# Scores of the first channel slot in two visits, and the middle angles of the first full theta slot ahead of its rotations

## The chip, the cores and the metric

The kernel runs on one core of a Trainium2 chip. The metric is device time in microseconds (us) for one execution. The kernel before takes 859.88 us, the median of three runs (858.89 to 861.0).

## The reference

```python
def _attn_ref(q, k, v, cap):                      # q, k, v: 8 x 12 heads x 448 x 64
    scores = cap * np.tanh(scale * q @ k.T / cap)
    attn = np.exp(scores - max); attn /= sum + 1e-09
    return attn @ v
def _moe_ref(x, w_theta, w_tok_r, w_tok_i, w_ch): # x: 8 x 448 x 768, the heads side by side
    theta = x @ w_theta
    y = w_tok_r @ (x * cos(theta)) + w_tok_i @ (x * sin(theta))
    u = x + y
    return u + np.maximum(u @ w_ch, 0.0)
```

Attention with capped scores feeds a block that turns each element by an angle `theta`, mixes along the tokens, adds, and ends in a channel matrix with a ReLU.

## The kernel before

Attention is cut into 24 slots of two pairs of heads each, so three slots make up one batch. A slot `s` makes the scores of its two pairs (words `S0` to `S3`), their tanh (`t0` to `t3`) and exp (`e0` to `e3`), and takes from slot `s-1` the product with V (`V0`, `W`, and the rest `Vr`), the row sums (`Ra`, `Rb`), their reciprocals (`I`) and the copies of the product out of PSUM (`cV0`, `cV1`). Into the same slots the second block is woven, four slots behind: a theta slot (`T` the matrix, `y` the angle in turns, `d` its reduction, `sc` sine and cosine, `r` the rotation, `f` a transpose, `D` the DMAs that carry the transposed piece across partitions), a mix slot (`h` and `l` halves of the data, `M` the token matrix, `m` the sum) and a channel slot (`u` halves of the data, `C` the matrix, `c` its output), each for six blocks of 128 channels.

Matrices are multiplied in three products of fp32r halves. The weights of the channel matrix come in twelve pieces, `ch0a` to `ch5b`, during slots 4 to 6: `@` loads a piece by two DMAs on POOL's queue, `*` scales it on ACT, `0` makes three DVE passes (L197, L198, L199), `1` one more DVE pass, and `2` casts the high half on ACT (L203, which waits for L198) and makes the low half on DVE (L204). Then its room goes back, and the load of a later piece that takes this room may start.

The order of the work is written by hand. `OTHER[s]` and `PARTS` are lists of words; `run` executes them one after the other, and this puts each word's instructions at the end of the queue of its engine. Engines run their queues in that order and wait for each other by semaphores. Slot 6 (`LEAD + 2`) is the first channel slot, slot 7 (`LEAD + 3`) the first theta slot behind it, slot 8 a mix slot from `PARTS`. The slots 5 and 6 are also those that split the channel weights.

PSUM has eight banks. Four go around in the pool `psM` (tag `m`) and hold one accumulator each (product, theta, mix, channel, sums); four belong to scores. Up to slot 6 the four are one tile: `S0`, `S1` and `S2` fill it one after the other, and one tanh of 1,792 columns empties it. From slot 7 on (`HALVES`, `once`) they are two tiles of two banks. There `S2` and `S3` take four banks of `psM` and one of the halves, so that all of `S1`, `S2`, `S3` stand in one visit, and the row sums lie in a bank of the score tile that `S1` fills afterwards. There, too, `cV1` runs on DVE instead of ACT, and the k halves of the second pair have rooms of their own.

Steps named later: `sums` (L491), `turn` (transposes the sums out of PSUM), `av_out` (the copies), `scores`, `tanh`, `prep_q`, `prep_k`, and `Split`/`Fields` for weights.

Of the kernel before, what the change touches and what calls it, by code (L numbers as in the profile page):

```python
# [28 lines left out]
LEAD = 4  # L29
# [10 lines left out]

FOLD = (0, 1, 2)

HALVES = LEAD + 3

FILL = {"branch": 10, "S0": 2, "t0": 8, "t1": 4}

# [34 lines left out]
def softcap_attn_then_spectral_mix(ctx, tc, qk2, v, cap, w_theta, w_tok, w_ch, outT):  # L81
# [9 lines left out]
    NS = B * NP2  # L91
# [191 lines left out]

    def once(s):
        return LEAD + 2 < s < NS

    def load_raw(k, part, last=False):
        t = raw[k, part] = small.take([P, S], F32, f"{'qk'[part]}{k}", None, int(part == 0 and once(k // 2) and (k // 2 - LEAD) % NP2 == 2), last)
        nc.sync.dma_start(t, qk2[k // NP, k % NP, :, part, :])
# [5 lines left out]
    def halves(t, shape, room, name, early):  # L295

        out = [room(shape, F32R, f"{name}{part}") for part in "hl"]
        (nc.scalar.copy if early else nc.vector.tensor_copy)(out[0], t)
        nc.vector.tensor_tensor(out[1], t, out[0].bitcast(F32), op=ALU.subtract)
        return out  # L300

    def by_scalar(k):
        return k < 2 * LEAD + 8 or k % 2 == 0 and (k // 2 - LEAD) % NP2 == 2

    def prep_q(k):

        if 2 * WHOLE <= k < 2 * NS:
            Q[k, "q"] = halves(raw[k, 0], [P, S], small.take, f"q{k}", by_scalar(k))
            if once(k // 2) and k % 2 and (k // 2 - LEAD) % NP2:
                Q[k, "rooms"] = [small.take([P, S], F32R, f"k{k}{part}") for part in "hl"]  # L310

    def prep_k(k, early=False):

        if 2 * WHOLE <= k < 2 * NS:
            t = raw[k, 1]
            if once(k // 2) and k % 2:
                if (k, "rooms") not in Q:
                    Q[k, "rooms"] = [small.take([P, S], F32R, f"k{k}{part}") for part in "hl"]
                rooms = iter(Q[k, "rooms"])
                Q[k, "k"] = halves(t[:, :REST], [P, REST], lambda shape, dtype, name: next(rooms)[:, :REST], f"k{k}", by_scalar(k))  # L320
            else:
                Q[k, "k"] = halves(t[:, :REST], [P, REST], lambda shape, dtype, name: wk.tile(shape, dtype, tag=f"k{name[-1]}", name=name, bufs=1), f"k{k}", by_scalar(k))
            if k % 2 == 0:
                Q[k, "r"] = wk.tile([P, S - REST], F32, tag="kr", name=f"r{k}", bufs=1)
                nc.vector.tensor_copy(Q[k, "r"], t[:, REST:])
            if early:
                Q[k, "early"] = True
            else:
                small.give(raw.pop((k, 1)))
            if k + 1 < 2 * NS:  # L330
                load_raw(k + 1, 1, k % 2 == 0 and by_scalar(k) and k > 2 * LEAD + 6)

    def scores(s, n):
        if once(s) and n >= 2:
            t = spt[s, n] = [psM.tile([P, 512], F32, tag="m", name=f"s{s}_{n}{h}") for h in range(2)]
            if n == 3:
                two = spt[s, "u"] = state["scores"].tile([P, 2, 512], F32, tag="s1", name=f"s{s}_u")
                chunk(s, (1, 2), [two[:, h] for h in range(2)])
            chunk(s, (1, n - 2), t)
        elif n == 3 and not once(s) and s not in (1, LEAD + 1):  # L340
            t = spt[s, n] = [psM.tile([P, 512], F32, tag="m", name=f"s{s}_{n}{h}") for h in range(2)]
            chunk(s, (1, 2), t)
        else:
            two = spt[s, n] = state.pop("two", None) if once(s) and n == 1 else None
            if not two:
                two = spt[s, n] = halves_of(s, n)
            for u, what in sorted(enumerate(BURSTS[n]), key=lambda at: at[1] is not None):
                chunk(s, what, [two[0][u][:, h] for h in range(2)])
        k = 2 * s + n // 2
        if n in ((1, 3) if s else (1, 2)) and s < WHOLE:  # L350
            for part in range(2):
                small.give(raw.pop((k, part)))
        elif s >= WHOLE and n % 2:
            for t in Q.pop((k, "q")) + (Q.pop((k, "rooms")) if (k, "rooms") in Q else []):
                small.give(t)
            if n == 1:
                for i in range(2):
                    small.give(raw.pop((k + i, 0)))
                if Q.pop((k + 1, "early"), False):
                    small.give(raw.pop((k + 1, 1)))  # L360
                if k + 2 < 2 * NS:
                    for i in range(2, 4):
                        load_raw(k + i, 0, once(s) and (s - LEAD) % NP2 == 2)

    def chunk(s, what, out):
        for i in (0, 1) if what is None else what[:1]:
            k = 2 * s + i
            rows, cols = (slice(i * D, (i + 1) * D), slice(REST, S)) if what is None else (slice(0, P), slice(what[1] * P, (what[1] + 1) * P))
            if what is None and (k, "r") in Q:
                products = ((Q.pop((k, "r")), raw[k, 0]),)  # L370
            elif what is None or s < WHOLE:
                products = ((raw[k, 1][:, cols], raw[k, 0]),)
            else:
                kk, qq = Q[k, "k"], Q[k, "q"]
                products = [(kk[a][:, cols], qq[c]) for a, c in (((0, 0), (0, 1), (1, 0)) if once(s) and i else ((0, 0), (1, 0), (0, 1)))]
            for m, (kk, qq) in enumerate(products):
                for h in range(2):
                    half = slice(h * D, (h + 1) * D)
                    nc.tensor.matmul(out[h][rows, :S], kk[half], qq[half], start=m == 0, stop=m == len(products) - 1)  # L379
# [317 lines left out]
    def chan_out(b, m):  # L697
# [190 lines left out]
```

## Time and profile before

| | |
|---|---|
| three runs | 858.89, 859.88, 861.0 us |
| profiled execution | 859.83 us, span 858.0 us |
| PE busy | 849.7 us (99% of the span), granted clock 0.999 |
| DVE, ACT, POOL busy | 720.7, 575.9, 116.0 us |
| chain that ended last, share of PE | 95% |

The span is what the trace covers, and the profiled execution's own time is 1.8 us longer. A timeline row gives the start in us, the time in us, the engine, the source line, the operation, output and inputs, and in brackets how long the engine stood idle before it and who released it. Several instructions may be merged in one row (`x8`); its time then runs from the first start to the last end. On one engine an instruction usually starts a little before its forerunner's end is recorded, so that the step from start to start is up to 0.1 us shorter than the recorded time.

### The profile page before, as it was taken

To read this page: it belongs to the slowest core of one execution; us is meant where nothing else is said; L and a number is where in the kernel's file an instruction comes from. 1 tells how busy PE (TensorE), PEld (TensorE's weight loads), DVE (VectorE), ACT (ScalarE), POOL (GpSimd) and SP (SyncE) were. 2 spreads that over 40 slices of the span, in tenths; PEclk is the share of its full clock that TensorE was granted. 3 is DMA by queue.
4 is the path that set the end of the run, shared out by engine and by line. 5 is a ranking of instruction groups with operands and counts; after the bars stand their busy time and mean duration, and the time that the engine had idled before them with its cause. 6 is when DMAs were issued, how large, how long until landed. Compare 5 with 4: busy or idle time off the path is not lost.

```text
span 858.0 us, 13327 instructions
## 1 busy us (share of the span) xinstructions
PE 849.7 (99%) x4756; PEld 646.1 (75%) x4756; DVE 720.7 (84%) x1168; ACT 575.9 (67%) x730; POOL 116.0 (14%) x244
## 2 busy tenths in 40 slices
PE   9999999999999999999999999999999999999997
PEld 4335676867878779778787797787787877879996
DVE  5988989999889898879998798897989979876741
ACT  6898987786873778727868468655787377824420
POOL 1121242201300032000310013000130003200300
PEclk9999999999999999999999999999999999999999
DMA  8686275741422324322423324134142332411401
GB/s 315 198 299 227 71 239 192 258 130 43 130 80 86 116 65 130 97 97 65 125 81 97 113 67 122 55 119 130 44 130 82 92 95 62 111 44 33 141 13 57
DMA packets 51692, 99.74 MB, mean 116 GB/s; under 512 B 11232, under 2 KB 42208, under 8 KB 51616
## 3 DMA queue, kind: packets, MB, share of 16 engines
q1 hardware_dynamic: 38880, 58.81, 22.1%
q0 software_dynamic: 9568, 29.89, 11.4%
q10 hardware_dynamic: 3168, 10.09, 3.9%
q8 instruction: 39, 0.64, 0.3%
q14 instruction: 37, 0.30, 0.1%
HBM read 54.72 MB, written 11.01 MB: 77 GB/s over the span
## 4 chain that ended last, share of the span: by engine, by line
PE 95%; DVE 2%; ACT 1%; issue 0%; SPq 0%; DMA 0%; ACTq 0%; POOL 0%; DVEq 0%; POOLq 0%
PE s L379 13%; PE a L483 13%; PE mx L684 8%; PE mx L686 8%; PE mx L685 8%; PE ch L583 7%; PE ch L584 7%; PE ch L585 7%; PE th L583 6%; PE th L585 6%; PE th L584 6%; PE a L477 2%; PE r L521 2%; PE s_u L379 1%; ACT p L405 1%; PE fill L130 1%
## 5 line engine op out<-in xcount | busy, mean ns | idle before, releaser
L653 POOL DMA_DIRECT2D t<-g_row x160 | 78.7, 499 | 531.5 <-ACT z L607 424.9
L684 PE MATMUL mx<-wtk_h,zh 128*128 128x448 f32 x336 | 124.1, 369 | 0.0
L686 PE MATMUL mx<-wtk_h,zl 128*128 128x448 f32 x336 | 123.4, 367 | 0.1
L685 PE MATMUL mx<-wtk_l,zh 128*128 128x448 f32 x336 | 123.0, 366 | 0.0
L425 ACT ACTIVATE p<-p,singles 128x1792 f32<-128x1792 f32 (+1 forms) x76 | 117.5, 1554 | 1.6 <-PE a L483 0.6
L583 PE MATMUL th<-xs,wth_h 128*128 128x448 f32 x288 | 106.1, 369 | 0.0
L583 PE MATMUL ch<-us,wch_h 128*128 128x448 f32 x288 | 105.9, 368 | 0.0
L584 PE MATMUL ch<-us,wch_h 128*128 128x448 f32 x288 | 105.9, 368 | 0.0
L584 PE MATMUL th<-xs,wth_h 128*128 128x448 f32 x288 | 105.5, 366 | 0.0
L585 PE MATMUL th<-xs,wth_l 128*128 128x448 f32 x288 | 105.5, 366 | 0.0
L585 PE MATMUL ch<-us,wch_l 128*128 128x448 f32 x288 | 105.4, 366 | 0.0
L483 PE MATMUL a<-p,v 128*64 128x448 f32 x492 | 101.8, 545 | 0.0
L411 ACT ACTIVATE p<-s,singles 128x896 f32<-128x896 f32 x34 | 32.4, 1004 | 91.5 <-PE s L379 91.4
L483 PEld LDWEIGHTS a<-p,v 128*64 128x64 f32 x492 | 32.9, 136 | 56.5 <-issue 51.4
L684 PEld LDWEIGHTS mx<-wtk_h,zh 128*128 128x128 f32 x336 | 63.1, 188 | 9.8 <-issue 2.5
L667 ACT CAST zh<-t 128x512 fp32r<-128x512 f32 x88 | 47.2, 563 | 31.1 <-PE mx L685 13.7
L686 PEld LDWEIGHTS mx<-wtk_h,zl 128*128 128x128 f32 x336 | 63.1, 188 | 6.4 <-DVE zl L674 1.1
L685 PEld LDWEIGHTS mx<-wtk_l,zh 128*128 128x128 f32 x336 | 63.1, 188 | 5.2
L674 DVE TENSOR_TENSOR zl<-t,zh 128x512 fp32r<-128x512 f32 x88 | 52.6, 611 | 12.8 <-ACT zh L667 11.2
L583 PEld LDWEIGHTS th<-xs,wth_h 128*128 128x128 f32 x288 | 54.0, 188 | 7.8 <-ACT p L408 1.9
L583 PEld LDWEIGHTS ch<-us,wch_h 128*128 128x128 f32 x288 | 54.0, 188 | 7.1 <-ACT p L408 1.6
L584 PEld LDWEIGHTS th<-xs,wth_h 128*128 128x128 f32 x288 | 54.0, 188 | 4.9 <-DVE xs L576 0.2
(718 smaller groups left out, 1704.6 us busy)
## 6 DMA issues: line engine op xcount, KB each, us to landing
v<-in_v ACTq DMA_DIRECT2D x22, 448.0 KB, 3.8
bc<-ri SPq DMA_DIRECT2D x88, 112.0 KB, 3.0
t<-g_row SPq DMA_DIRECT2D x160, 56.0 KB, 2.4
t<-g_row POOLq DMA_DIRECT2D x160, 56.0 KB, 2.2
q<-in_qk SPq DMA_DIRECT2D x39, 224.0 KB, 3.2
k<-in_qk SPq DMA_DIRECT2D x39, 224.0 KB, 3.9
out_dram<-x SPq DMA_DIRECT2D x34, 224.0 KB, 1.9
x_row<-in_qk SPq DMA_DIRECT2D x18, 224.0 KB, 2.9
```

What stands on the lines that cost most here:

```text
L379: nc.tensor.matmul(out[h][rows, :S], kk[half], qq[half], start=m == 0, stop=m == len(products) - 1)
L425: nc.scalar.activation(pp, pp, AF.Exp, scale=cap_sb)
L483: nc.tensor.matmul(acc_of["a", s, i][h * D : (h + 1) * D, :S], vt[s][:, 6 * i + 3 * h + c, :], U[s, (i, c)][:, h, :], start=first and c == ...
L583: nc.tensor.matmul(acc[:, :S], wh[:, j, ms], t[:, 0, :], start=j == 0, stop=False)
L584: nc.tensor.matmul(acc[:, :S], wh[:, j, ms], t[:, 1, :], start=False, stop=False)
L585: nc.tensor.matmul(acc[:, :S], wl[:, j, ms], t[:, 0, :], start=False, stop=j == NJ - 1)
L653: queue.dma_start(t[32 * m : 32 * m + 32, d * S : (d + 1) * S], f[32 * d : 32 * d + 32, m * S : (m + 1) * S])
L667: nc.scalar.copy(zh.rearrange("p c (d x) -> p c d x", x=32), tokens(b, j)[:, c0:c1])
L674: nc.vector.tensor_tensor(zl, tokens(b, j)[:, c0:c1], zh.bitcast(F32), op=ALU.subtract)
L684: nc.tensor.matmul(acc[:, :S], zh, wtk_h[:, c, :], start=c == 0, stop=False)
L685: nc.tensor.matmul(acc[:, :S], zh, wtk_l[:, c, :], start=False, stop=False)
L686: nc.tensor.matmul(acc[:, :S], zl, wtk_h[:, c, :], start=False, stop=c == NC2 - 1)
```

## The change

Slot 6 is handled as the later ones are: `HALVES` and `once` begin one slot earlier. Its four score banks are two tiles, `S1`, `S2` and `S3` come in one visit ahead of `C0`, the sums of slot 5 lie in a score bank, and `cV1` of slot 5 runs on DVE. The lists of slots 5 to 7 are rewritten for it: the second pair's q and k are split at the slot's start, and the steps of the channel weights are set at other places among the words. In slot 7 the words `T3 y3 d2 d3 sc1 T4 y4` now stand ahead of `r0 r1 f0 f1 D0`, and `F1` ahead of `d4`.

```diff
-HALVES = LEAD + 3
+HALVES = LEAD + 2
...
     def once(s):
-        return LEAD + 2 < s < NS
+        return LEAD + 1 < s < NS
...
-            if k + 1 < 2 * NS:
+            if k + 1 < 2 * NS and k != 2 * HALVES + 1:
                 load_raw(k + 1, 1, k % 2 == 0 and by_scalar(k) and k > 2 * LEAD + 6)
...
                 if k + 2 < 2 * NS:
+                    if s == HALVES:
+                        load_raw(k + 2, 1)
                     for i in range(2, 4):
...
-        LEAD + 2: "S0 t0 :1ch2a :2ch2a :@ch3b V0 u5 e0 :*ch2b :0ch2b W Ra Rb Vr cV0 cV1 v :1ch2b :2ch2b :@ch4a :*ch3a :0ch3a Pa1 S1 Pb1 q0 t1 :1ch3a :2ch3a :@ch4b :*ch3b C0 I c0 :0ch3b :1ch3b a0a e1 :2ch3b :@ch5a :*ch4a C1 :0ch4a :@ch5b"
+        LEAD + 2: "Pa1 S0 t0 Pb1* V0 e0 :*ch2b W Ra Rb Vr cV0 S1 cV1 :0ch2a :1ch2a :2ch2a :@ch3b t1 u5 :0ch2b S2 S3 :1ch2b :2ch2b :@ch4a :*ch3a t2 v :0ch3a q0 I a0a e1 :1ch3a :2ch3a :@ch4b :*ch3b a0b t3 C0 :0ch3b c0 :1ch3b :*ch4a :2ch3b :@ch5a C1 :0ch4a :@ch5b"
...
+        LEAD + 3: "Pa1 S0 t0 Pb1* V0 e0 N- Yh4 Yh5 W Ra Rb Vr cV0 S1 Yl0 Yl1 Yl2 cV1 t1 S2 S3 Yl3 Yl4 Yl5 v w0 q0 I w1 a0a Pa0 Pb0 q1 t2 Pa3 e1 a0b T0 y0 t3 N d0 e2 F0 Pb3* T1 y1 e3 d1 a1a sc0 a1b T2 y2 T3 y3 d2 d3 sc1 T4 y4"
+        " r0 r1 f0 f1 D0 F1 d4 T5 y5 r2 r3",
```

ACT's queue in slot 6, before. `s6_0`, `s6_1` are score tiles, `p6` the tanh and exp of slot 6, `a5` the product of slot 5, `us` the halves for the channel matrix, and `swc` and `g_row` the rooms of weight pieces (here `swc2a` is ch2a, `g_row` ch2b, `swc3a` ch3a).

```order
L405 ACTIVATE p6_0_1272<-s6_0_1259,singles_64 128x1792 [waits PE_49]
L203 CAST wch_h_73<-swc2a0_1175 128x3x128 [waits DVE_49]
L574 CAST us0_4_1253<-x2_1_532 128x448
L425 ACTIVATE p6_0_1272<-p6_0_1272,singles_64 128x1792 [waits Activation_49]
L153 ACTIVATE g_row_79<-g_row_79 128x384 [waits DMASW4_49]
L488 COPY x_row_80<-a5_0_1280 128x448 [waits PE_49]
L488 COPY x5_1_1311<-a5_1_1294 128x448 [waits PE_49]
L293 DMA v6_1313<-in_v 128x896
L203 CAST wch_h_73<-g_row_79 128x3x128 [waits DVE_49]
L153 ACTIVATE swc3a0_1256<-swc3a0_1256 128x384 [waits DMASW6_49]
L298 CAST q13h_1324<-q13_1154 128x448 [waits DMAHW0_49]
```

The same stretch of ACT's queue now, from the copy of the product to the tanh of `S2` (`s6_20`).

```order
L490 COPY x5_0_1312<-a5_0_1284 128x448 [waits PE_49]
L203 CAST wch_h_73<-swc2a0_1173 128x3x128 [waits DVE_49]
L413 ACTIVATE g_row_79<-s6_11_1301,singles_64 128x896 [waits PE_49]
L413 ACTIVATE g_row_79<-s6_10_1300,singles_64 128x896 [waits PE_49]
L576 CAST us0_4_1249<-x2_1_532 128x448
L203 CAST wch_h_73<-g_row_79 128x3x128 [waits DVE_49]
L153 ACTIVATE swc3a0_1252<-swc3a0_1252 128x384 [waits DMASW6_49]
L410 ACTIVATE p6_2_1375<-s6_20_1346,singles_64 128x448 [waits PE_49]
L410 ACTIVATE p6_2_1375<-s6_21_1347,singles_64 128x448 [waits PE_49]
```

The cast of ch2a moved behind the copy of the product and ahead of `t1`, and the last `us` cast, the cast of ch2b and the scaling of ch3a stand between `t1` and `t2`.

DVE's queue over the same time, before:

```order
L576 TENSOR_TENSOR us0_2_1232<-x_row_80,us0_2_1232 128x448 [waits Activation_49]
L197 TENSOR_SCALAR swc2a0_1175<-swc2a0_1175 128x384 [waits DMASW2_49,Activation_49]
L198 SCALAR_TENSOR_TENSOR swc2a0_1175<-swc2a0_1175 128x384 [waits DVE_49]
L199 TENSOR_SCALAR swc2a0_1175<-swc2a0_1175 128x384 [waits DVE_49]
L576 TENSOR_TENSOR us0_4_1253<-x2_0_495,us0_4_1253 128x448 [waits Activation_49]
L201 TENSOR_SCALAR swc2a0_1175<-swc2a0_1175 128x384 [waits DMASW3_49]
L204 SCALAR_TENSOR_TENSOR wch_l_74<-swc2a0_1175 128x3x128 [waits DVE_49]
L576 TENSOR_TENSOR us0_4_1253<-x2_1_532,us0_4_1253 128x448 [waits Activation_49]
L197 TENSOR_SCALAR g_row_79<-g_row_79 128x384 [waits DMASW4_49,Activation_49]
```

and now:

```order
L531 STREAM_TRANSPOSE ri5_1306<-s6_10_1300 128x448 [waits PE_49]
L490 COPY x_row_80<-a5_1_1293 128x448 [waits PE_49]
L197 TENSOR_SCALAR swc2a0_1173<-swc2a0_1173 128x384 [waits DMASW2_49]
L198 SCALAR_TENSOR_TENSOR swc2a0_1173<-swc2a0_1173 128x384 [waits DVE_49]
L199 TENSOR_SCALAR swc2a0_1173<-swc2a0_1173 128x384 [waits DVE_49]
L201 TENSOR_SCALAR swc2a0_1173<-swc2a0_1173 128x384 [waits DMASW3_49]
L204 SCALAR_TENSOR_TENSOR wch_l_74<-swc2a0_1173 128x3x128 [waits DVE_49]
L578 TENSOR_TENSOR us0_4_1249<-x2_1_532,us0_4_1249 128x448 [waits Activation_49]
L197 TENSOR_SCALAR g_row_79<-g_row_79 128x384 [waits DMASW4_49]
L198 SCALAR_TENSOR_TENSOR g_row_79<-g_row_79 128x384 [waits DVE_49]
```

The passes over ch2a moved behind two instructions that wait for PE, the transpose of the sums and the copy of the second product.

DVE's queue in slot 7, before: `z1_0` are the angles of blocks 0 and 1, `z1_2` of 2 and 3, `z1_4` of 4 and 5, and `ft7_1` is the fold `F1` of the row sums.

```order
L629 TENSOR_TENSOR z1_0_1754<-z1_0_1754,x_row_80 128x896 [waits Activation_49]
L629 TENSOR_TENSOR z1_0_1754<-z1_0_1754,x3_1_659 128x896
L637 STREAM_TRANSPOSE g_row_79<-z1_0_1754 128x7x4x32 [waits DVE_49] x2
L613 SCALAR_TENSOR_TENSOR z1_2_1824<-z1_2_1824 128x448 [waits Activation_49]
L614 TENSOR_SCALAR z1_2_1824<-z1_2_1824 128x448 [waits DVE_49]
L616 TENSOR_SCALAR z1_2_1824<-z1_2_1824 128x448 [waits DVE_49]
```

and now:

```order
L615 SCALAR_TENSOR_TENSOR z1_2_1830<-z1_2_1830 128x448 [waits Activation_49]
L616 TENSOR_SCALAR z1_2_1830<-z1_2_1830 128x448 [waits DVE_49]
L618 TENSOR_SCALAR z1_2_1830<-z1_2_1830 128x448 [waits DVE_49]
L631 TENSOR_TENSOR z1_0_1760<-z1_0_1760,x_row_80 128x896
L631 TENSOR_TENSOR z1_0_1760<-z1_0_1760,x3_1_659 128x896
L639 STREAM_TRANSPOSE g_row_79<-z1_0_1760 128x7x4x32 [waits DVE_49] x2
L458 STREAM_TRANSPOSE ft7_1_1905<-ps7_1_1805 128x896
L459 TENSOR_REDUCE folds_78<-ft7_1_1905 128x28 [waits DVE_49]
L615 SCALAR_TENSOR_TENSOR z1_4_1881<-z1_4_1881 128x448 [waits Activation_49]
```

The two reductions of `z1_2` moved ahead of the rotations and transposes of `z1_0`, and the fold ahead of the reduction of `z1_4`.

## Rows read from the trace of the kernel before

**Rows 1.** The page: busy us of each engine, and the granted clock in 40 slices.

```profile
PE 849.7 (99%) x4756; PEld 646.1 (75%) x4756; DVE 720.7 (84%) x1168; ACT 575.9 (67%) x730; POOL 116.0 (14%) x244
PEclk9999999999999999999999999999999999999999
```

**Rows 2.** Timeline of PE, slots 7 and 8: start, time, line, operation, idle before.

```profile
179.57 0.98 PE L477 MATMUL a<-g_row,v 64*64 64x448 f32 x8
180.37 0.54 PE L379 MATMUL s<-q,r 64*64 64x448 f32 x1
...
182.57 0.37 PE L379 MATMUL s_u<-q15h,k15h 64*128 64x448 f32 x2
...
183.88 0.47 PE L583 MATMUL th<-xs,wth_h 128*128 128x448 f32 x1
...
206.16 0.47 PE L379 MATMUL s<-q16h,k16h 64*128 64x448 f32 x2
...
213.40 0.30 PE L497 MATMUL s<-folds,diagonal 128*64 128x28 f32 x4 [1.08 <-issue]
...
217.03 0.47 PE L379 MATMUL s_u<-q17h,k17h 64*128 64x448 f32 x2 [0.25 <-ACT g_row L411]
```

**Rows 3.** Timeline of PE, slot 6 and the start of slot 7.

```profile
145.62 0.98 PE L477 MATMUL a<-g_row,v 64*64 64x448 f32 x8
146.43 0.54 PE L379 MATMUL s<-q,r 64*64 64x448 f32 x1
...
172.60 0.47 PE L379 MATMUL s<-q14h,k14h 64*128 64x448 f32 x2
```

**Rows 4.** Timeline of ACT, slots 6 and 7.

```profile
144.63 0.57 ACT L203 CAST wch_h<-swc2a 128x384 fp32r<-128x384 f32 x1 [2.43 <-DVE swc2a L198]
145.11 0.56 ACT L574 CAST us<-x 128x448 fp32r<-128x448 f32 x1
...
147.27 0.53 ACT L153 ACTIVATE g_row<-g_row 128x384 f32<-128x384 f32 x1
...
180.59 0.53 ACT L488 COPY x<-a 128x448 f32<-128x448 f32 x1 [0.82 <-PE a L477]
181.37 1.01 ACT L411 ACTIVATE p<-s,singles 128x896 f32<-128x896 f32 x1 [0.25 <-PE s L379]
...
183.17 0.63 ACT L408 ACTIVATE p<-s,singles 128x448 f32<-128x448 f32 x1
```

**Rows 5.** Timeline of DVE, slot 6: passes over ch2a and a `us` subtraction.

```profile
143.65 0.35 DVE L197 TENSOR_SCALAR swc2a<-swc2a 128x384 int32<-128x384 int32 x1
144.04 0.56 DVE L198 SCALAR_TENSOR_TENSOR swc2a<-swc2a 128x384 int32<-128x384 int32 x1
144.64 0.37 DVE L199 TENSOR_SCALAR swc2a<-swc2a 128x384 int32<-128x384 int32 x1
144.91 0.62 DVE L576 TENSOR_TENSOR us<-x,us 128x448 fp32r<-128x448 f32 x1
145.45 0.35 DVE L201 TENSOR_SCALAR swc2a<-swc2a 128x384 int32<-128x384 int32 x1
145.84 0.58 DVE L204 SCALAR_TENSOR_TENSOR wch_l<-swc2a 128x384 fp32r<-128x384 uint32 x1
```

**Rows 6.** Timeline of DVE, slot 6: the last pass over the channel weights (ch5b).

```profile
169.52 0.56 DVE L204 SCALAR_TENSOR_TENSOR wch_l<-swc5b 128x384 fp32r<-128x384 uint32 x1
```

**Rows 7.** Timeline of DVE, slot 7: the first passes of `d2` and of `d4`.

```profile
205.19 0.58 DVE L613 SCALAR_TENSOR_TENSOR z<-z 128x448 f32<-128x448 f32 x1
...
207.94 0.62 DVE L613 SCALAR_TENSOR_TENSOR z<-z 128x448 f32<-128x448 f32 x1
```

**Rows 8.** The chain that ended last, 196 to 222 us: the last piece of `D0`.

```profile
209.71 2.30 DMA t<-g_row
```

**Rows 9.** Timeline of ACT, slot 8.

```profile
214.08 1.55 ACT L667 CAST zh<-t 128x512 fp32r<-128x512 f32 x3
...
215.95 1.03 ACT L411 ACTIVATE g_row<-s,singles 128x896 f32<-128x896 f32 x1
```

More of the change, by code (lines that the diff above doesn't have):

```diff
@@ L721, in softcap_attn_then_spectral_mix @@
         " S2 t2 M2a h3a l3a a0a M2b h3b l3b :@ch1b m1 M3a h4a l4a :*ch1a :0ch1a M3b h4b l4b a0b e2 m2 :1ch1a S3 q1 t3 M4a h5a l5a :2ch1a :@ch2a m3 M4b"
-        " h5b l5b Pa0 Pb0 :*ch1b :0ch1b a1a u0 u1 e3 :1ch1b M5a :2ch1b :@ch2b m4 u2 M5b a1b m5 u3 :*ch2a :0ch2a u4 :@ch3a",
-        LEAD + 2: "S0 t0 :1ch2a :2ch2a :@ch3b V0 u5 e0 :*ch2b :0ch2b W Ra Rb Vr cV0 cV1 v :1ch2b :2ch2b :@ch4a :*ch3a :0ch3a Pa1 S1 Pb1 q0 t1 :1ch3a :2ch3a :@ch4b :*ch3b C0 I c0 :0ch3b :1ch3b a0a e1 :2ch3b :@ch5a :*ch4a C1 :0ch4a :@ch5b"
-        " S2 S3 t2 :1ch4a :2ch4a :*ch4b t3 c1 :0ch4b a0b C2 :*ch5a :1ch4b :2ch4b e2 :0ch5a :*ch5b C3 c2 :1ch5a :2ch5a :0ch5b :1ch5b :2ch5b a1a Pa0 Pb0 q1 N- c3 C4 e3 a1b c4 Xh0 Xh1 Xh2 Xh3 C5 c5",
-        LEAD + 3: "Pa1 S0 t0 Pb1* V0 e0 N- Yh4 Yh5 W Ra Rb Vr cV0 S1 Yl0 Yl1 Yl2 cV1 t1 S2 S3 Yl3 Yl4 Yl5 v w0 q0 I w1 a0a Pa0 Pb0 q1 t2 Pa3 e1 a0b T0 y0 t3 N d0 e2 F0 Pb3* T1 y1 e3 d1 a1a sc0 a1b T2 y2 r0 r1 f0 f1 D0 T3 y3 d2"
-        " d3 T4 y4 d4 sc1 F1 T5 y5 r2 r3",
+        " h5b l5b Pa0 Pb0 :*ch1b :0ch1b a1a u0 u1 e3 :1ch1b M5a :2ch1b :@ch2b m4 u2 M5b a1b m5 u3 :*ch2a u4 :@ch3a",
+        LEAD + 2: "Pa1 S0 t0 Pb1* V0 e0 :*ch2b W Ra Rb Vr cV0 S1 cV1 :0ch2a :1ch2a :2ch2a :@ch3b t1 u5 :0ch2b S2 S3 :1ch2b :2ch2b :@ch4a :*ch3a t2 v :0ch3a q0 I a0a e1 :1ch3a :2ch3a :@ch4b :*ch3b a0b t3 C0 :0ch3b c0 :1ch3b :*ch4a :2ch3b :@ch5a C1 :0ch4a :@ch5b"
+        " :1ch4a :2ch4a :*ch4b c1 :0ch4b C2 :*ch5a :1ch4b :2ch4b e2 :0ch5a :*ch5b C3 c2 :1ch5a :2ch5a :0ch5b :1ch5b :2ch5b a1a Pa0 Pb0 q1 N- c3 C4 e3 a1b c4 Xh0 Xh1 Xh2 Xh3 C5 c5",
+        LEAD + 3: "Pa1 S0 t0 Pb1* V0 e0 N- Yh4 Yh5 W Ra Rb Vr cV0 S1 Yl0 Yl1 Yl2 cV1 t1 S2 S3 Yl3 Yl4 Yl5 v w0 q0 I w1 a0a Pa0 Pb0 q1 t2 Pa3 e1 a0b T0 y0 t3 N d0 e2 F0 Pb3* T1 y1 e3 d1 a1a sc0 a1b T2 y2 T3 y3 d2 d3 sc1 T4 y4"
+        " r0 r1 f0 f1 D0 F1 d4 T5 y5 r2 r3",
         NS: "u0 u1 Vr V0 u2 u3 u4 u5 W cV0 cV1 Ra Rb I C0 c0 X0 X1 C1 c1 X2 X3 C2 c2 N X4 X5 T0+ y0+ d0+ T1+ y1+ d1+ sc0+ T2+ r0+ r1+ f0+ f1+ D0+ y2+ d2+ T3+"
```

## Prediction

> **What bounds the kernel now.** I read the page's busy times first: PE is busy 849.7 of 858.0 us at the full granted clock, its higher level of 2.4 GHz [rows 1]. So an edit on another engine counts only where PE waits for it, and a gain can only come out of PE's own idle time or its own instructions. Second I read PE's timeline through slots 6 to 8. Slot 6 has no idle time at all; behind it PE stands for 1.08 us ahead of the sums in slot 8 and for 0.25 us ahead of `s_u` there [rows 2]. Third come ACT's and DVE's timelines over the same stretch, for what their queues hold at the places where PE will now ask for them [rows 4, 5, 7, 9].
>
> **What can be gained.** In slot 7 the three visits `S1` to `S3` already stand together: from the first matmul of `S1` at 180.37 to the first theta matmul at 183.88 they take 3.51 us, and 108 matmuls of a matrix follow in 22.28 us, to 206.16 [rows 2]. Slot 6 with the same order would start `S1` at 146.43 as before and end at 146.43 + 3.51 + 22.28 = 172.22 instead of 172.60 [rows 3]: 0.38 us less, for one break fewer in PE's stream. The other possible gain is the idle 1.08 + 0.25 us of slot 8 [rows 2]. Both together are 1.71 us, and no more than that can be won.
>
> **What the new order makes PE wait for, slot 6.** Two of PE's steps now hang on ACT. `s_u` writes into the banks of `s6_11` and so waits for the first tanh of `t1`. `C0` takes the `psM` bank of `s6_20` and so waits for the first tanh of `t2`. In slot 7 nothing stands in ACT's queue between these tanhs but a DMA issue, and the two of `t1` and the first of `t2` follow on each other: `t1` starts at 181.37, `t2` at 183.17 [rows 4]. In slot 6 the casts of the weights stand between them, and each cast waits for DVE. I follow the two queues, from start to start:
>
> - The product's rest starts at 145.62 [rows 3]. In slot 7 a copy of it starts 180.59 - 179.57 = 1.02 us after its rest [rows 2, 4], with ACT waiting. So the copies start at 146.64, `cV0` on ACT and `cV1` on DVE.
> - DVE: the copy is of one width with the `us` subtraction, whose step is 145.45 - 144.91 = 0.54 [rows 5]; so the passes over ch2a start at 147.18. From the first of them to the cast on ACT there are 144.63 - 143.65 = 0.98 us [rows 4, 5]: cast at 148.16. ACT has stood idle for it. The row of before shows just this wait, 2.43 us on the same cast, where no PE step was behind it [rows 4].
> - ACT: a cast takes 145.11 - 144.63 = 0.48 [rows 4], so `t1` starts at 148.64 and its first tanh ends 1.01 later [rows 4], at 149.65. `s_u` in slot 8 starts 0.05 after the tanh that frees it (215.95 + 1.03 = 216.98 against 217.03) [rows 2, 9], so here at 149.70. Without the wait it would stand 182.57 - 180.37 = 2.20 behind `S1` [rows 2], at 148.63. **First wait: 1.07 us.**
> - The two tanhs of `t1` take 183.17 - 181.37 = 1.80 [rows 4]: at 150.44 ACT comes to the last `us` cast, 0.56 [rows 4], done at 151.00. DVE has finished with ch2a at 147.18 + (146.42 - 143.65 with the `us` step of 0.54 taken out) = 149.41 [rows 5] and stands, because its next instruction is the subtraction of that very `us`. It runs at 151.03 and takes 0.54; ch2b's passes start at 151.57, and 0.98 later, at 152.55, ACT may cast ch2b. Then 0.48 for this cast and about 0.44 for the scaling of ch3a (0.53 recorded, less the 0.09 by which the cast's step is shorter than its record) [rows 4]: `t2` starts at 153.47. Its first tanh takes 0.63 [rows 4], and with 0.05 as above `C0` starts at 154.15. After `s_u` at 149.70 it could have started 183.88 - 182.57 = 1.31 later [rows 2], at 151.01. **Second wait: 3.1 us.**
> - `C0` to `C5` take 22.28 us from there, to 176.43, against 172.60 [rows 3]: slot 6 is 3.8 us longer, with the 0.38 us of the merged visit in it.
>
> Behind the waiting casts on ACT stand `t2`, `e1` and `t3`, behind the waiting subtraction on DVE all later weight passes. The loads follow them: a piece's room is loaded again when its passes are over, so ch3b's load starts as much later as ch2a's end, 149.41 against 145.84 + 0.58 = 146.42 [rows 5], that is 3.0 us, and ch5a's load waits in turn for ch3b's room, with ch5b's behind it. Before, the last pass over ch5b ended at 169.52 + 0.56 = 170.08 [rows 6]. Moved by 3.0 us it ends at 173.1. `C5` would now start at 176.43 - 22.28/6 = 172.72 and wants ch5b in its second half, 1.86 us on, at 174.6. The cover holds with 1.5 us to spare, so I cost it at nothing; without the cover it is a rival below.
>
> What is added beside this stands on engines that wait anyhow: four more tanhs (the same columns in more pieces, on ACT ahead of 146.64 or behind `C0`), and one copy that passes from ACT to DVE, which is in the sum above. The q and k halves of the second pair come earlier on both engines, before the transpose of the sums, and that transpose must free its bank by 147.3 or so: it follows the sums at once and takes no term.
>
> **Slots 7 and 8.** All of slot 7's start shifts with PE, since DVE's transpose of the sums waits for PE there. Within the slot, `sc1` no longer has to wait for the rotations; ACT gets to `t0` of slot 8 earlier, so the 1.08 us ahead of the sums go. But `D0`'s DMAs start when the two transposes end, and ahead of these now stand the reductions `d2` and `d3`, 207.94 - 205.19 = 2.75 us [rows 7]. The last piece landed at 209.71 + 2.30 = 212.01 [rows 8], so on the old clock now at 214.76. ACT's cast of it stood at 214.08 without a wait [rows 9], and ahead of the copies and of `t1`. It now starts between 214.76 and 215.2 (ACT also works through the semaphores of sixteen DMAs), that is 0.7 to 1.1 us later, and `t1` and `s_u` behind it as well: 217.7 to 218.1 instead of 217.03. The wait moves from the sums to `s_u`, and the slot's net is a loss of 0.7 to 1.1 us; I take 0.8. If DVE or the DMAs make up the 2.75 us it is a gain of 1.33, and this is the other end.
>
> **Sum.** 859.83 (profiled) + 3.8 + 0.8 = 864.4 us, +0.5%. The profiled execution is within 0.05 us of the median of the runs, so 864.4 is the forecast of the median too. Its own range, from tenths on each step of the two chains, is 863.4 to 865.6.
>
> **Rivals.**
>
> *The waits don't come (not slower).* If `t2` reached ACT by 150.3, PE would find `C0`'s bank free, as `T0` does in slot 7 [rows 2, 4]. For this DVE would have to serve both casts without the `us` subtraction holding it, or `C0` another bank. Then 0.38 is won in slot 6, and with 1.33 in slot 8 the time is 858.1. For it speaks slot 7, which has this order and no idle time; against it that slot 7 has no casts among its tanhs. A half of it (only the second wait goes, and slot 8 loses nothing) gives about 860.5. Chance 18%, in 5 of which the time is under 857.3.
>
> *PE's clock falls.* PE stands still for 3.1 us in one piece, shortly after 1.1. No row here shows such a stretch, nor the lower level. If the clock went down to 1.2 GHz and came back within one `C` block, that block would take 3.7 us more (22.28/6, once more) [rows 2]: 868.1. For it: the longest idle time of this trace behind its first microseconds is a third as long. Against it: at 1.08 us nothing happened. Chance 10%.
>
> The Trainium skill, in "TensorE: Matmul & The Clock Gate", Part 1 on the clock gate, says that an idle array is throttled to half its clock until it has been busy again for a time. By that rule this rival's time would hold if the pause is long enough; no run here shows it so far.
>
> *The weights come late.* If the loads of ch3b, ch5a and ch5b lose more than the 1.5 us of cover, for example because they now fall among the q and k loads, `C5` waits too, by 1 to 2 us: 866. For it speaks that ch5b was done only 0.7 us before its use (`C5` from 172.60 - 3.71 = 168.89, its second half from 170.75, against 170.08) [rows 3, 6]; against it that PE's own wait gives them 3.8 us. Chance 10%.
>
> **Chances and range.** Forecast 62%, no waits 18%, clock 10%, weights 10%. A difference under 0.3% (2.6 us) can't be told from none with this kernel. Slower by more than that: 82%; the same: 13%; faster: 5%. The range from 861.5 to 868.5 holds the forecast, the late weights and the clock, and the edge of the first rival.
>
> **What would show it.** In the profile after, slot 6 must have two idle stretches of PE, about 1 us ahead of `s_u` and about 3 us ahead of `C0`, both released by ACT tanhs, with ACT idle ahead of the casts of ch2a and ch2b and DVE idle ahead of a `us` subtraction. Slot 8 must have no wait ahead of the sums and one of about 2 us ahead of `s_u`. If `C0` follows `S3` at once, the sum is wrong at its largest term. If PE stands and the total is the same, something later gave the time back. If the `C` matmuls run at double pitch, it was the clock.

## The result, and the profile after

The changed kernel takes 869.77 us, the median of four runs (868.42 to 870.03), against 859.5 for the kernel before beside it. The ratio is 1.0116, with a 95% interval of 1.0101 to 1.0131. It is slower, as forecast, but by 10.3 us and not by 4.5, and it lies above the whole range of 861.5 to 868.5. The profiled execution is the fastest of the four: 868.42 us, span 866.6, against 859.83 and 858.0 before, so the accounts below explain 8.6 us. Ratios here are of fast runs alone; the one slow run on record took 3667.11 us, with slot 7's change alone, and is left out of that kernel's figures below.

First the page after: busy time of each engine, and the granted clock in 40 slices.

```profile
PE 852.1 (98%) x4756; PEld 649.1 (75%) x4756; DVE 721.2 (83%) x1169; ACT 576.4 (67%) x733; POOL 116.5 (13%) x244
PEclk9999999899999999999999999999999999999999
```

PE has the same 4,756 matmuls as in [rows 1], but is busy 2.4 us longer, out of 8.6, and one slice shows a lower clock. So the loss is partly idle time and partly slower work. Idle time stands in the view of waits: engine, line, who was waited for, us in total, times, longest.

```profile
PE ch L585 <- ACT p L410: 3.0, 1, 3.0
PE s L381 <- DVE folds L538: 2.9, 1, 2.9
PE s_u L381 <- ACT g_row L413: 1.7, 1, 1.7
```

The first and the third are the two waits forecast for slot 6. The second was not forecast; it lies in slot 8. PE's timeline through slot 6 shows what stands behind the waits (start, time, line, operation, idle before).

```profile
145.98 0.54 PE L381 MATMUL s<-x_row,r 64*64 64x448 f32 x1
...
146.38 0.54 PE L381 MATMUL s<-x_row,k 64*64 64x448 f32 x1
...
149.99 0.47 PE L381 MATMUL s_u<-q13h,k13h 64*128 64x448 f32 x2 [1.66 <-ACT g_row L413]
...
154.42 0.74 PE L585 MATMUL ch<-us,wch_h 128*128 128x448 f32 x1 [2.95 <-ACT p L410]
154.96 0.57 PE L586 MATMUL ch<-us,wch_h 128*128 128x448 f32 x1
155.33 0.57 PE L587 MATMUL ch<-us,wch_l 128*128 128x448 f32 x1
...
158.98 0.36 PE L585 MATMUL ch<-us,wch_h 128*128 128x448 f32 x1
159.18 0.37 PE L586 MATMUL ch<-us,wch_h 128*128 128x448 f32 x1
```

`S1` starts 0.45 us earlier than in [rows 3] (146.43); this difference is there before slot 6 begins. After the second wait `C0` runs at a step of 0.37 (154.96 to 155.33), and from 158.98 on at 0.20. The windows name the cause: us of PE, PEld, DVE, ACT and POOL busy, granted clock, DMA share, GB/s, in slot 6 and then in slot 8.

```profile
150.00:154.40 4.40, 1.46 (x12) 1.03 (x12) 2.95 (x8) 2.84 (x6) 1.08 (x2) 0.73 0.79 252
154.40:156.00 1.60, 1.58 (x4) 1.45 (x5) 1.53 (x4) 1.60 (x2) 1.08 (x2) 0.50 0.67 246
156.00:158.00 2.00, 2.00 (x7) 1.74 (x7) 1.97 (x4) 2.00 (x4) 0.00 (x0) 0.50 0.99 273
158.00:160.00 2.00, 2.00 (x9) 1.82 (x8) 1.97 (x3) 1.74 (x4) 1.08 (x2) 0.78 0.96 312
...
222.00:224.00 2.00, 0.98 (x8) 0.94 (x10) 1.88 (x5) 2.00 (x4) 0.00 (x0) 0.93 0.00 0
224.00:226.00 2.00, 2.00 (x14) 1.76 (x14) 1.97 (x4) 1.06 (x3) 1.25 (x3) 0.50 0.28 63
```

Clock 0.50 is TensorE's lower level, 1.2 GHz. It comes once with each long pause: in slot 6 it begins inside the pause (the mean of 150.00 to 154.40 is 0.73) and lasts until about 158.9, in slot 8 it begins at about 223.7 and lasts until about 227.1.

ACT's and DVE's timelines in slot 6 show how the waits arise. ACT first:

```profile
146.19 0.53 ACT L490 COPY x<-a 128x448 f32<-128x448 f32 x1 [1.15 <-PE a L479]
148.47 0.56 ACT L203 CAST wch_h<-swc2a 128x384 fp32r<-128x384 f32 x1 [1.75 <-DVE swc2a L198]
148.93 1.90 ACT L413 ACTIVATE g_row<-s,singles 128x896 f32<-128x896 f32 x2
150.72 0.56 ACT L576 CAST us<-x 128x448 fp32r<-128x448 f32 x1
152.84 0.56 ACT L203 CAST wch_h<-g_row 128x384 fp32r<-128x384 f32 x1 [1.56 <-DVE g_row L198]
...
153.75 1.14 ACT L410 ACTIVATE p<-s,singles 128x448 f32<-128x448 f32 x2
```

And DVE:

```profile
146.94 0.62 DVE L490 COPY x_row<-a 128x448 f32<-128x448 f32 x1 [0.95 <-PE s L381]
...
147.88 0.56 DVE L198 SCALAR_TENSOR_TENSOR swc2a<-swc2a 128x384 int32<-128x384 int32 x1
...
151.32 0.63 DVE L578 TENSOR_TENSOR us<-x,us 128x448 fp32r<-128x448 f32 x1 [1.62 <-ACT us L576]
```

ACT stands 1.75 us ahead of the cast of ch2a and 1.56 ahead of that of ch2b, DVE 1.62 ahead of the `us` subtraction between them: the chain as it was forecast. The one row that is off is DVE's copy. It starts at 146.94, released by PE's score matmuls, and not beside ACT's copy at 146.19. The first eight matmuls of `S1` read `x_row`, into which the copy writes, and the last of them ends at 146.38 + 0.54 = 146.92.

In slot 8 the wait ahead of the sums [rows 2] is gone, and a longer one stands in the second half of `S1`. PE:

```profile
223.01 0.47 PE L381 MATMUL s<-q16h,k16h 64*128 64x448 f32 x2 [2.87 <-DVE folds L538]
...
224.10 0.58 PE L381 MATMUL s<-q17l,k17h 64*128 64x448 f32 x2
...
227.20 0.47 PE L686 MATMUL mx<-wtk_h,zh 128*128 128x448 f32 x1
```

DVE, on which PE waits:

```profile
221.38 1.11 DVE L639 STREAM_TRANSPOSE g_row<-z 128x896 f32<-128x896 f32 x1 [1.74 <-DMA t<-g_row]
222.42 0.19 DVE L537 TENSOR_SCALAR folds<-s,singles 128x14 f32<-128x14 f32 x1
222.73 0.23 DVE L538 SCALAR_TENSOR_TENSOR folds<-s,singles,folds 128x14 f32<-128x14 f32 x1
```

ACT:

```profile
221.26 1.55 ACT L669 CAST zh<-t 128x512 fp32r<-128x512 f32 x3 [3.91 <-DMA t<-g_row]
223.14 1.01 ACT L413 ACTIVATE g_row<-s,singles 128x896 f32<-128x896 f32 x1
```

`f2`'s transpose (221.38) writes the room from which `D0`'s DMAs read, so it waits for them. The masking of the folded sums (L537, L538) stands behind it on DVE, and PE waits for the masking.

By slots, from one start of `S0` on PE to the next:

| us | before | after | difference |
|---|---|---|---|
| up to slot 6 | 138.65 | 138.21 | -0.44 |
| slot 6 | 33.95 | 40.48 | +6.53 |
| slot 7 | 33.56 | 33.56 | 0 |
| slot 8 | 38.51 | 40.91 | +2.40 |
| rest | 613.33 | 613.44 | +0.11 |

Slot 6, from start to start as the forecast counts: `s_u` stands 4.01 us behind `S1` instead of 2.20 (+1.81) and `C0` 4.43 behind `s_u` instead of 1.31 (+3.12). In these are the waits of 1.66 and 2.95; the other 0.32 are slower starts behind the pauses. `C0` to `C5` take 24.27 instead of 22.28, their first part at the lower clock (+1.99), and the merged visit saves 0.38. Slot 8: from `S0` to `S1` 6.97 us instead of 8.27, with the old wait of 1.08 gone; from `S1` to the mix 7.98 instead of 4.02; the mix 25.96 instead of 26.22. In the 7.98 are the 3.51 of [rows 2], the new wait of 2.87 and 1.60 more, nearly all for matmuls at the lower clock.

### The profile page after: what moved, and what is told of

Same layout as the page of the kernel before. It is cut to its first block, busy times and chain, and to the rows that moved or that the text cites. A ratio compares the mean times of both kernels' runs of the same rounds, so it can differ in the third digit from the quotient of the medians.

```text
span 866.6 us, 13325 instructions
## 1 busy us (share of the span) xinstructions
PE 852.1 (98%) x4756; PEld 649.1 (75%) x4756; DVE 721.2 (83%) x1169; ACT 576.4 (67%) x733; POOL 116.5 (13%) x244
## 4 chain that ended last, share of the span: by engine, by line
PE 94%; DVE 3%; ACT 1%; issue 1%; SPq 0%; DMA 0%; DVEq 0%; POOL 0%; POOLq 0%
PE s L381 12%; PE a L485 12%; PE mx L686 8%; PE mx L688 8%; PE mx L687 8%; PE ch L585 7%; PE ch L587 7%; PE ch L586 7%; PE th L585 6%; PE th L586 6%; PE th L587 6%; PE a L479 2%; PE r L523 1%; PE s_u L381 1%; ACT p L407 1%
## 5 line engine op out<-in xcount | busy, mean ns | idle before, releaser
L413 ACT ACTIVATE p<-s,singles 128x896 f32<-128x896 f32 x36 | 34.3, 1005 | 91.4 <-PE s L381 91.4
L585 PEld LDWEIGHTS ch<-us,wch_h 128*128 128x128 f32 x288 | 54.7, 190 | 9.6 <-ACT p L410 4.9
L585 PEld LDWEIGHTS th<-xs,wth_h 128*128 128x128 f32 x288 | 54.0, 188 | 7.8 <-ACT p L410 1.9
L586 PEld LDWEIGHTS ch<-us,wch_h 128*128 128x128 f32 x288 | 54.6, 190 | 4.9
```

Of the source, the lines that this page charges most:

```text
L585: nc.tensor.matmul(acc[:, :S], wh[:, j, ms], t[:, 0, :], start=j == 0, stop=False)
L586: nc.tensor.matmul(acc[:, :S], wh[:, j, ms], t[:, 1, :], start=False, stop=False)
```

## The experiments

The theory: two queues make PE stand. In slot 6 it is ACT's, where the casts that wait for DVE stand ahead of the tanhs; in slot 8 it is DVE's, where `f2` waits for `D0`'s room. Each pause of about 3 us then costs again by the lower clock. The rivals: the loss of slot 8 is one that slot 6 hands on; the slow matmuls come of the crowd of loads and weight passes in slot 6 and not of the pause.

### Each half of the change alone

The first kernel has the change without its new list of slot 7. The second has only that list.

```diff
 slot 6 alone (against the kernel after): the list of slot 7 is the old one
-... T2 y2 T3 y3 d2 d3 sc1 T4 y4 r0 r1 f0 f1 D0 F1 d4 T5 y5 r2 r3
+... T2 y2 r0 r1 f0 f1 D0 T3 y3 d2 d3 T4 y4 d4 sc1 F1 T5 y5 r2 r3
 slot 7 alone (against the kernel before): the list of slot 7 is the new one
-... T2 y2 r0 r1 f0 f1 D0 T3 y3 d2 d3 T4 y4 d4 sc1 F1 T5 y5 r2 r3
+... T2 y2 T3 y3 d2 d3 sc1 T4 y4 r0 r1 f0 f1 D0 F1 d4 T5 y5 r2 r3
```

> The slots 5 and 6 of the change alone; slot 7 keeps the word order of before. Theory (the weight casts ahead of t1 and t2 hold PE twice, 1.66 and 2.95 us, the clock falls in the second pause and costs 2.0 us more; slot 8's loss comes from D0's later start in slot 7 and not from here): slot 6 lasts 40 to 41 us against 33.95, slot 8 about 38.5 as before, so 6.0 to 6.8 us over the kernel before, about 866 us. Rival (slot 8's longer wait is handed on by slot 6): slot 8 is near 41 us and the total 8 to 10 us over before.

> Slot 7's new word order alone; slots 5 and 6 as before. Theory (D0 starts 2.75 us later, the next transpose into the room that D0 reads waits for its DMAs, and the masking of the folded sums stands behind that transpose on DVE, so that PE waits some 2.9 us inside S1 and its clock falls again): slot 8 is 1 to 2.7 us longer than before, 860.5 to 862.3 us. Rival (the reordering does what it can gain, the wait ahead of the sums goes and nothing else comes): 1.0 to 1.4 us under before.

Slot 6 alone takes 866.44 us (866.19 to 867.01), ratio 1.0083 with 1.0058 to 1.0108. Its waits:

```profile
PE ch L585 <- ACT p L410: 3.0, 1, 3.0
PE s_u L381 <- ACT g_row L413: 1.9, 2, 1.7
PE s L499 <- issue: 1.1, 1, 1.1
```

Both waits of slot 6 are there, and slot 6 takes 40.33 us. Slot 8 takes 38.54, as before, with its old wait of 1.1 ahead of the sums.

Slot 7 alone takes 861.70 us, the median of nine runs (860.85 to 862.63), ratio 1.0026 with 1.0014 to 1.0038. PE in its slot 8:

```profile
216.32 0.74 PE L379 MATMUL s<-q16h,k16h 64*128 64x448 f32 x2 [2.90 <-DVE folds L536]
216.86 0.57 PE L379 MATMUL s<-q16h,k16l 64*128 64x448 f32 x2
217.23 0.57 PE L379 MATMUL s<-q16l,k16h 64*128 64x448 f32 x2
```

Slot 8 takes 41.03 us here, behind an undisturbed slot 6. So each half has its own loss, 6.7 and about 2.0 us by the medians, and nothing is handed on. Together they are 8.7 us, which fits the 8.6 of the traces; the 10.3 between the medians of the whole change are 1.6 more, and no run explains these. The lower clock follows this pause too (step 0.37), where slot 6's weight loads are long over: the DMA engines' share is 0.04 from 216 to 218.

### The pause filled with other matmuls

Slot 6 alone, and after `S3` matmuls of 32 by 112 into a free score bank, whose result nothing uses: 24 in one kernel, 14 in the other.

```diff
+    def keep_busy(n):
+        t = state["scores"].tile([P, 2, 512], F32, tag="s0", name="busy")
+        for _ in range(n):
+            nc.tensor.matmul(t[:32, 0, :112], ..., start=True, stop=True)
...
+                if s == LEAD + 2 and word == "S3":
+                    keep_busy(24)    # the other kernel: 14
```

> As slot6_only, with 24 small matmuls into a free score bank between S3 and C0, which keep PE busy for about 2.6 us while it would wait; their output is used by nothing. Theory (the half-rate matmuls at the start of C0 follow from the pause): C0 starts when it did, within 0.3 us, its matmuls are at the 0.206 us step from the first, the granted clock stays 1.00 through C0, and the total is 1.6 to 2.2 us under slot6_only. Rival (the matmuls of C0 are slowed by the weight DMAs, which take 0.99 of the DMA engines just then): C0 lasts about 5.7 us as in slot6_only and the total is the same as there.

> As busy_wait, with 14 of the small matmuls instead of 24; since each is recorded as two of 0.10 us, they take about 2.8 us, no longer than the pause. Theory (pause, then half rate): C0 starts within 0.3 us of where slot6_only has it, measured from S0 of the slot, C0 to C5 take 22.1 to 22.4 us at full clock instead of 24.11, and the total is 1.6 to 2.2 us under slot6_only. Rival (the weight DMAs slow the matmuls, and busy_wait escaped them because its C0 came 2.4 us later): C0 to C5 take 23 us or more although PE never paused.

With 24 of them, 866.24 us: no change in sum against slot 6 alone (866.44). The trace shows each of them as two, 48 times 0.10 = 4.8 us, longer than the pause, so `C0` starts 18.00 us after `S0` instead of 16.22; but `C0` to `C5` take 22.16 us, not 24.11. The total alone decides nothing. With 14 the extra work just fits the pause; PE in slot 6:

```profile
152.12 0.47 PE L386 MATMUL s_u<-q13h,k13h 64*128 64x448 f32 x2 [1.66 <-ACT g_row L418]
...
153.53 2.92 PE L135 MATMUL busy<-singles 128*32 128x112 f32 x28
156.56 0.47 PE L590 MATMUL ch<-us,wch_h 128*128 128x448 f32 x1
156.87 0.37 PE L591 MATMUL ch<-us,wch_h 128*128 128x448 f32 x1
157.07 0.37 PE L592 MATMUL ch<-us,wch_l 128*128 128x448 f32 x1
```

`C0` starts 16.21 us after `S0`, as without the filling (16.22), and goes at once at a step of 0.20. `C0` to `C5` take 22.27 us instead of 24.11, slot 6 takes 38.48 instead of 40.33, and the whole 864.03 us (ratio 1.0043, 1.0028 to 1.0059). The loads, the passes and the first wait of 1.66 are the same in both kernels, so the slow matmuls come of the long pause: 1.84 us of slot 6. The rival of the crowded slot falls.

### The tanhs ahead of the weight steps

Slot 6 alone, but `u5` ahead of the product, and all passes over ch2a and ch2b and the scaling of ch3a behind `t2`.

```diff
-... Pb1* V0 e0 :*ch2b W Ra Rb Vr cV0 S1 cV1 :0ch2a :1ch2a :2ch2a :@ch3b t1 u5 :0ch2b S2 S3 :1ch2b :2ch2b :@ch4a :*ch3a t2 v :0ch3a ...
+... Pb1* u5 V0 e0 :*ch2b W Ra Rb Vr cV0 S1 cV1 t1 S2 S3 t2 :0ch2a :1ch2a :2ch2a :@ch3b :0ch2b :1ch2b :2ch2b :@ch4a :*ch3a v :0ch3a ...
```

> As slot6_only, but the last us cast stands ahead of V0 and all passes over ch2a and ch2b, and the scaling of ch3a, stand behind t2. Theory (only the queue order of ACT and DVE makes PE wait): both pauses of PE in slot 6 go to under 0.3 us each, the clock stays at its upper level, and the total is 859 to 861 us, with up to 1 us if the weights now come late for C5. Rival (the single visit of S1 to S3 in this slot can't be fed by ACT, whatever the order): pauses of 1 us and more stay ahead of s_u or C0, and the total is above 863 us.

860.19 us (859.67 to 862.02), ratio 1.0010 with 1.0000 to 1.0020. PE's waits in slot 6:

```profile
PE ch L585 <- ACT p L403: 0.7, 1, 0.7
PE ch L585 <- ACT wch_h L203: 0.3, 1, 0.3
```

Both pauses are gone, the granted clock stays at 1.00, and `C0` starts 11.29 us after `S0` instead of 16.22. In their place stand two small waits: `C2` for `t3`, which still stands behind the weight steps, and `C5` for a weight. Slot 6 takes 35.08 us, still 1.1 more than before. So the order of the two queues, ACT's and DVE's, is the cause of the large waits (this run moved steps in both), and the cover of the weights, which held in the kernel after, is used up here.

### The wait in slot 8

Both kernels are slot 7 alone, with one thing changed: `f2` gets a room of its own, or `r0` to `D0` stand ahead of the reductions `d2`, `d3` again.

```diff
 a room of its own
-..., FLIP if 0 < b and (b < B - 1 or j != 2) else None, last=b == 0)
+..., FLIP if 0 < b and (b < B - 1 or j != 2) and (b, j) != (1, 2) else None, last=b == 0)
 the carry first
-... T2 y2 T3 y3 d2 d3 sc1 T4 y4 r0 r1 f0 f1 D0 F1 d4 T5 y5 r2 r3
+... T2 y2 T3 y3 r0 r1 f0 f1 D0 d2 d3 sc1 T4 y4 F1 d4 T5 y5 r2 r3
```

> As slot7_only, but the second transpose of slot 8 (f2, f3) writes into another room than the one D0 is read from. Theory (the masking of the folded sums is late because it stands behind a transpose that waits for that room): PE's wait ahead of the second half of S1 falls from 2.9 to under 1 us; D0's data still come late for ACT, so that t1 and s_u wait instead, 1.2 to 2.2 us; slot 8 lasts 38.8 to 40 us against 41.03 and 38.5. Rival (DVE's queue is late by itself, whatever room it writes): the wait stays at 2.5 us or more at the same place.

> As slot7_only, but r0 r1 f0 f1 D0 stand ahead of d2 d3 again, with sc1 ahead of T4 y4 and F1 ahead of d4 as in the change. Theory (all of slot 8's loss is D0's later start): no wait of PE on the folds; what stays is the wait of before ahead of the sums, up to 1.2 us; total within 1 us of the kernel before. Rival (sc1, F1 and y4 at their new places cost too): slot 8 stays 1 us or more longer than 38.5.

With the room of its own, 866.75 us (864.39 to 868.66), ratio 1.0089 with 1.0073 to 1.0104: 7.4 us over the kernel before where slot 7 alone was 2.0 over it. Slot 8 takes 45.08 us, where 38.8 to 40 were expected. PE's waits:

```profile
PE mx L684 <- ACT p L408: 3.2, 1, 3.2
PE s_u L379 <- ACT g_row L411: 1.5, 1, 1.5
PE s L379 <- DVE folds L536: 1.0, 1, 1.0
```

and what ACT stood for in it:

```profile
213.93 1.55 ACT L667 CAST zh<-t 128x512 fp32r<-128x512 f32 x3 [3.92 <-DMA t<-g_row]
...
222.04 1.16 ACT L408 ACTIVATE p<-s,singles 128x448 f32<-128x448 f32 x2 [5.21 <-DMA t<-f]
```

The wait for the folds falls from 2.9 to 1.0, so the room was the cause of 1.9 us of it. In the 1.0 that stays DVE is no later than before: the masking ends 8.86 us after `S0`, in the kernel before 8.88. PE, which no longer waits ahead of the sums, is there earlier. The wait of 1.5 us ahead of `s_u` is the one that the prediction expected: ACT waits 3.92 us for `D0`'s data, and `t1` stands behind. The 3.2 us are another matter. By the code the pool now gives the room that `f2` wrote, the one from which the next carry, `D1`, reads (`t<-f`), to the tile of `t2`; so ACT waits for the DMAs of `D1`, and the mix matmuls wait for ACT. The kernel thus shows what the shared room cost, but it is no measure of what its removal is worth.

With the carry first, 860.55 us (859.39 to 863.12), ratio 1.0018 with 1.0007 to 1.0029. The wait for the folds is gone. The one ahead of the sums is not:

```profile
214.25 0.30 PE L497 MATMUL s<-folds,diagonal 128*64 128x28 f32 x4 [2.14 <-issue]
```

It was 1.08. `sc1` now stands ahead of `y4`, and ACT comes later to the table load for `t0`: 5.89 us after `S0` of slot 8 (211.85), against 4.83 before (210.99).

Slot 8 takes 39.57 us, 1.06 more than before, which is just how much later ACT comes. So of the 2.52 us that the new list costs in slot 8, 1.46 go when `D0` stands ahead of `d2` and `d3` again, and 1.06 stay. ACT's rows put these on `sc1` at its new place; no run moved it alone. The rival holds beside the theory, and the total is 1.2 us over the kernel before and not within 1.

### The best of these

Slot 6 with the tanhs first, `t3` moved up and one pass over ch2a back in slot 5; slot 7 of the kernel before with `T5 y5` ahead of `d4 sc1 F1`; in slot 8 the row sums (`Ra`, `Rb`) ahead of `f2`.

```diff
-... a0a e1 :1ch3a :2ch3a :@ch4b :*ch3b a0b t3 C0 ...
+... a0a e1 t3 :1ch3a :2ch3a :@ch4b :*ch3b a0b C0 ...
-... T4 y4 d4 sc1 F1 T5 y5 r2 r3
+... T4 y4 T5 y5 d4 sc1 F1 r2 r3
-V0 f2 W Ra Rb f3
+V0 W Ra Rb f2 f3
```

> A version meant to win: slot 6 as in tanh_first, with ch2a's first passes back at the end of slot 5 and t3 right behind e1; slot 7 in the order of before but with T5 y5 ahead of d4 and sc1; in slot 8 the sums ahead of f2, so that neither the room of D0 nor the late t0 holds PE. Theory: no pause of PE over 0.5 us in slots 6 to 8, slot 6 about 33.6 us and slot 8 37.2 to 37.8 us: 858.0 to 858.8 us, 0.1 to 0.2% under before. Rival (each wait removed uncovers the next, as tanh_first did at C2 and C5): within 0.5 us of the kernel before.

859.5 us (858.94 to 861.58), ratio 1.0008 with 0.9999 to 1.0017: no gain. Slot 6 takes 34.46 us and slot 8 38.80, 0.5 and 0.3 above the kernel before. The largest waits of PE in slots 6 to 8:

```profile
PE s L381 <- DVE ri L531: 0.4, 1, 0.4
PE s_u L381 <- ACT g_row L413: 0.3, 1, 0.3
```

So the rival holds: each wait that goes leaves smaller ones that it had covered. No version that ran beats the kernel before.

## Why the prediction was wrong in size

Right: the direction, and that PE waits for ACT twice in slot 6. The second one delays `C0` by 3.12 us (forecast 3.1; 2.95 of them show as idle time), and the merged visit's 0.38 us is in the account. No `C` matmul waited for a weight, so that cover held at no cost. The wait ahead of the sums vanished. `D0`'s data reached ACT at 221.26, inside the 220.85 to 221.29 that the forecast gives when it is moved to this slot's start.

Wrong, by the steps of the sum:

- **The clock.** The rival at 10% came true, and twice. The prediction held against it that nothing happened at 1.08 us; but it forecast a pause of 3.1 us itself, for which no row spoke either way, and then left the clock out of the sum. It cost 1.99 us in slot 6 and nearly all of 1.60 in slot 8 (in the 2.4 below), some 3.5 together. The Trainium skill, "TensorE: Matmul & The Clock Gate", Part 1 on the clock gate, says that an idle array drops to half its clock; the traces agree, with a granted clock of 0.50. With 10% on this rival the range ended at 868.5, and it had the clock fall in one place alone, at a price of 3.7 us. That its 868.1 comes near the 868.42 of the profile is luck: the place that it meant cost 1.99, and the rest came from slot 8 and the first wait.
- **Slot 8, +2.4 instead of +0.8.** The step that failed is "the wait moves from the sums to `s_u`". The prediction followed `D0`'s lateness to its one reader on ACT and forgot who writes next into the room that `D0` reads. That is `f2`, on DVE, ahead of the masking that PE needs. The wait was 2.87 us, released at 222.96, and it came before the one forecast at `s_u`, which it covers; where the wait for the room was taken away, that one showed, with 1.54 us. The other end of the forecast, a gain of 1.33 us, was not there either: with the wait ahead of the sums gone, PE comes to the masking 1.0 us before it is done, as the run with the room of its own shows.
- **The first wait in slot 6, 1.81 instead of 1.07** (1.66 of them idle time). "So the copies start at 146.64" took ACT's copy in slot 7 for both. DVE's copy came 0.75 us behind ACT's, released by score matmuls and not by the product, and everything on the chain behind it shifted with it. In slot 7 before, DVE came to its copy too late for any wait to show. The cause is again a room: by the code `cV1` runs behind `S1` and takes the room in `x_row` that the raw q of slot 6's first pair has just given back, and the first eight matmuls of `S1` read it. The copy starts 0.02 us after the last of them ends. No run gave the copy another room, so this is read from code and rows and not tested.

With the three steps as measured the forecast becomes 859.83 + 3.8 + 0.7 + 2.0 + 2.4 = 868.7 us; less the 0.3 us of the stretches ahead of slot 6 and behind slot 8 it is 868.4, as profiled. The median of 869.77 lies another 1.3 us higher; the trace of one execution doesn't say why.

## What to carry to other kernels

When a step is moved ahead in a queue, look for three things behind it: the instruction that now waits at the queue's head, the steps of other engines that stand behind it, and whoever writes next into a room that a delayed DMA or a matmul still reads. When a forecast holds a TensorE pause longer than any in the trace, price the lower clock behind it too, one time for each such pause. A wait that is taken out is worth only the difference to the next one behind it.

## What the hardware showed that was not expected

- The clock was 0.50 after pauses of 2.87, 2.90, 2.95 and 2.96 us: in slot 6 the pause came 1.5 us behind one of 1.66, in slot 8 alone. With 2.14 us in one piece (the carry first) it stayed at 1.00 in the traced execution, here in the pause and behind it:

```profile
212.00:214.30 2.30, 0.16 (x4) 0.08 (x3) 2.30 (x4) 2.29 (x3) 0.00 (x0) 1.00 0.00 0
214.30:216.00 1.70, 1.70 (x20) 0.70 (x20) 1.58 (x5) 1.70 (x4) 0.00 (x0) 1.00 0.00 0
```

- Only one execution of each kernel was traced. With slot 7 alone the mean granted clock was 0.996 or 0.997 in the four longest executions (862.04 to 862.63 us) and 0.998 or 0.999 in the other five (860.85 to 861.70); with the carry first it was 0.996 or 0.997 in five of ten, the three longest (862.48 to 863.12) among them. So the same pause may bring the lower level in one execution and not in the next; this is not shown.
- The lower level also came with two shorter pauses: with the room of its own PE stood 1.01 us, worked 1.5, stood 1.54 until 216.88 and was then at 0.50:

```profile
218.00:220.00 2.00, 1.48 (x8) 0.78 (x6) 1.17 (x2) 0.00 (x0) 1.50 (x4) 0.50 0.70 202
```

- The lower level need not begin with the first matmul behind the pause. In slot 6 it began inside the pause. In slot 8 of the kernel after, matmuls went at full pitch from 223.01 and only from about 223.7 at half of it; in slot 7 alone the first one was slow.
- Matmuls whose result nobody uses kept the clock up: 3.0 us of them in the pause were worth 1.84 us behind it.
